# Loads of q and k head by head, one token per partition, ahead of the block transposes of an attention and MLP kernel

## The chip, the cores and the metric

The kernel runs on one core of a Trainium2 chip. The time is the device time of one execution in microseconds, the median of several runs: 353.92 us for the kernel before (3 runs, 352.54 to 354.34). TensorE (PE) multiplies matrices, VectorE (DVE) and ScalarE (ACT) work on elements, GpSimd (POOL) here mostly issues the loads that also cast fp32 to bf16, and SyncE (SP) issues the stores.

## The reference

Causal attention with a sliding window of 64 tokens, for 8 batches, 8 heads, 576 tokens and a head size of 64; its result, 4608 tokens of 512, goes through two dense layers with a SiLU between them.

```python
scores = (q @ k.transpose(0, 1, 3, 2)) / sqrt(64)
scores = where(0 <= i - j < 64, scores, -1e9)
attn = softmax(scores)
x = (attn @ v).transpose(0, 2, 1, 3).reshape(4608, 512)
h = x @ w_in                       # 512 -> 2048
out = (h * sigmoid(h)) @ w_out     # 2048 -> 512
```

All inputs and the output are fp32; the kernel computes in bf16 with fp32 accumulation.

## The kernel before

**Attention by batch.** A score matmul needs q and k with the head dimension on partitions. For batch 0 the transposes are done by TensorE (`turn_first`). For batches 1 to 7 they are done by VectorE in blocks of 32 by 32 (`turn_blocks`, L247): the head dimension is cut into two halves of 32, so that the four heads of a group fill 128 partitions, and the scores of one head are the sum of two matmuls over 32 rows (`scores`, L333). A batch has two groups of four heads (a = 0, 1), each with q and k, and each of these four tensors of [4 heads, 576 tokens, 64] takes one load (`load_four`, L240) into a buffer `nat` and two transposes, one per half of the columns.

The load of before gives partition p the p-th of 128 equal pieces of the flat tensor. 32 partitions hold one head, and a partition holds 18 consecutive tokens (NR = 18), 1152 elements in a row. Token number 18 t + r of a head lies in partition t of its 32, at row r. A block transpose takes one r, and its 32 output columns t belong to tokens 18 t + r, so they are written into `qt` or `kt` with a step of 18 elements.

After the scores of three blocks of 64 tokens for all 8 heads (a unit; three units a batch, g = 0 to 2) come the exponential on ScalarE (L339), a multiplication with the window's mask on VectorE (L342), the matmul with v (`values`, L351), the division by the row sums (`inverse` L358, `normal` L361), and a block transpose that puts the result into `bridge` with the model dimension on partitions (L365). v is loaded by GpSimd in four parts per batch (L254), and VectorE copies half of it by 64 partitions (`shift_v`, L299 and L301).

**The two dense layers by tile.** A tile is 512 tokens; there are nine. The first layer (L371) has 16 groups of four matmuls over 512 columns, each followed by a SiLU on ScalarE (L377); the second layer (L380) has four outputs of 16 matmuls each, each copied out (L386) and stored. Tile 0 splits its first FIRST = 8 groups into token ranges 0 to 192 and 192 to 512, so that work can begin when the first unit of batch 0 is done. A batch has 576 tokens, so tile j needs batches 0 to j, and of batch j only its first 512 - 64 j tokens.

**What sets the order.** The class `Plan` is a list scheduler that runs when the kernel is built. Each piece of work is added with a class, an assumed cost in microseconds on each engine that may do it, its dependences and, for PSUM users, a pool of banks. `Plan.run` simulates the engines with those costs and always takes the ready head of the class with the best rank. The result is a fixed order of instructions per engine; on the chip an engine waits at its next instruction, whatever stands behind it. The cost assumed for one block transpose is 0.7 us. Scores are held back by `scores_may_run` so that they stand between the second-layer matmuls of the tile before: during the second layer of tile j TensorE also does the scores and values of batch j + 1.

**Queues.** All loads except two go through GpSimd's one DMA queue in the order in which GpSimd issues them; there are eight semaphores for them, so an issue waits until the DMA eight places ahead has landed. At the start these are: q and k and v of batch 0, w_in in ten loads, then q and k of batch 1 (four loads), then w_out and v of batch 1 in the order of SECOND_LOADS = "wvvwvv" (w is one part of w_out, v one part of v) with the remaining parts of w_out, then q, k and v of batch 2 and so on. There are eight `nat` buffers, so the loads of batch b wait until the transposes of batch b - 2 have read theirs; there are two `qt` and two `kt`, so the transposes of batch b wait for the scores of batch b - 2; there are three buffers for v.

Of the kernel before, what the change touches and what calls it, by code (L numbers as in the profile page):

```python
# [122 lines left out]
def kernel(ctx, tc, q, k, v, w_in, w_out, out):  # L123
    nc = tc.nc
    B, H, S, D = q.shape
# [1 line left out]
    assert (B, H, S, D) == (8, 8, 576, 64) and (d_model, d_ff) == (512, 2048)  # L127
    NP = H // 2
    NB = S // 64
    NR = H * S * D // 2 // 128 // D  # L130
    NG = 3
    NDC = d_model // 128
    NFT = d_ff // 128
    TT = 512
# [1 line left out]
    TB = TT // 64  # L136
    NK = 2
    NN, NNB, NE, NOT, NGT = 8, 8, 12, 4, NFT + 3
    FIRST, SECOND_LOADS = 8, "wvvwvv"
    FIRST_LOADS = [(x[0], int(x[1])) for x in "q0 k0 q1 k1 q2 q3 k2 k3 v0 v1 v2 v3".split()]  # L140
    NOX, NRC, NV = 6, 6, 3
    NIV = 2
    NM0, MARGIN = 9, 1.3
# [16 lines left out]
    nats = [keep.tile([128, 2 * S], BF16, name=f"nat{i}") for i in range(NN)]  # L160
# [15 lines left out]
    p = Plan(  # L176
        {"at": range(4), "pv": range(4, 6), "mp": range(4, 8), "all": range(8)},
        rank=dict(prime=-8, early=-10, one=-9, first=-9, dma=-1, ld0=-1, st=-2, silu=-3, out=-2, pv=0, s=1, moe=99, warm=200, turn=2,
                  norm=0, inverse=0, bridge=0, exp=1, mask=1, lift=2, block=2, shift=2, cast=4, late=5, clear=9),
        rank0=dict(turn=-6, cast=-6, lift=-5, shift=-4.5, exp=-4, mask=-4, inverse=-3.5, norm=-3, bridge=-3.2),  # L180
        ahead=dict(s=-5.5, exp=-4.6, pv=-5.5, inverse=-4.3, norm=-4.2, bridge=-4.25),
    )
# [27 lines left out]
    def clear_vv(i):  # L210
        nc.vector.memset(vv[i][:, :, D:D + 1], 1.0)
        nc.vector.memset(vv[i][0:64, 0, 0:D], 0.0)
# [5 lines left out]
    c_vv = [p.add("one", {"DVE": 0.25}, lambda _, i=i: clear_vv(i)) for i in range(NV)]  # L218
# [17 lines left out]
        copies[e](out=natbs[w][:, 0:S], in_=nats[i][:, 0:2 * S].bitcast(FP32))  # L236


    def load_four(i, b, a, kk):
        nc.gpsimd.dma_start(  # L240
            out=nats[i], in_=(q, k)[kk][b, 4 * a:4 * a + 4].rearrange("h s d -> (h s d)").rearrange("(p x) -> p x", p=128))

    def turn_blocks(i, b, a, kk, part):

        n = NR // 2
        to = kt[b % NK][:, 64:] if kk else qt[b % NK]
        nc.vector.transpose(  # L247
            out=to[:, 2 * a * S:2 * a * S + 2 * S].rearrange("x (s t r) -> x r s t", s=2, r=NR)[:, n * part:n * part + n],
            in_=nats[i].rearrange("p (r s d) -> p r s d", r=NR, s=2)[:, n * part:n * part + n],
        )  # L250

    def load_v(e, b, part):
        g0, g1 = part * 9, part * 9 + 9
        queue[e].dma_start(  # L254
            out=vv[b % NV][:, 2 * g0 + 1:2 * g1 + 1:2, 0:D],
            in_=v[b].rearrange("h s d -> (h s) d").rearrange("(g p) d -> p g d", p=128)[:, g0:g1],
        )
# [7 lines left out]
    def load_w_out(f):  # L265
        nc.gpsimd.dma_start(
            out=w_out_sb[:, 2 * f:2 * f + 2, :],
            in_=w_out[f * 256:(f + 1) * 256, :].rearrange("(c p) m -> p c m", p=128),
        )
# [100 lines left out]
    def first_layer(bank, j, ft, c, lo, hi):  # L370
        nc.tensor.matmul(  # L371
            banks[bank["bank"][0]][:, lo:hi], lhsT=w_in_sb[:, c, ft * 128:(ft + 1) * 128],
            rhs=bridge[:, (j * TT + lo) // 64:(j * TT + hi) // 64, c], start=(c == 0), stop=(c == NDC - 1),
        )

    def silu(bank, gt, lo, hi):
        nc.scalar.activation(out=gts[gt][:, lo:hi], in_=banks[bank["bank"][0]][:, lo:hi], func=ACTF.Silu)  # L377

    def second_layer(bank, gt, m, f, lo, hi):
        nc.tensor.matmul(  # L380
            banks[bank["bank"][0]][:, 0:hi - lo], lhsT=gts[gt][:, m * 128:(m + 1) * 128], rhs=w_out_sb[:, f, lo:hi],
            start=(f == 0), stop=(f == NFT - 1),
        )
# [9 lines left out]
    win, wout = [], []  # L393
    v_landed = {}
    kq_done, v_done, s_last, pv_last = {}, {}, {}, {}
    nat_free = {}
    g_pv, g_norm, g_bridge, g_mask, o_done = [], [], [], [], {}
    moe = []
# [13 lines left out]
    n_nat = [0, 0]  # L412
# [30 lines left out]
    def add_w_out(which):  # L443
        wout.extend(p.add("dma", {"POOL": 0.75}, lambda _, f=f: load_w_out(f), dma=1.29, lat=MARGIN) for f in which)

    def add_batch_qk(b):
        busy = s_last.get(b - NK, []) + ([c_k[b % NK]] if b < NK else [])
        for a in range(2):
            kq_done[(b, a)] = []
            for kk in range(2):  # L450
                i = n_nat[0] % NN
                n_nat[0] += 1
                ld = p.add("dma", {"POOL": 0.66}, lambda _, i=i, a=a, kk=kk: load_four(i, b, a, kk), nat_free.get(i, []),
                           dma=1.7, lat=MARGIN)
                nat_free[i] = [p.add("block", {"DVE": 0.7}, lambda _, i=i, a=a, kk=kk, part=part: turn_blocks(i, b, a, kk, part),
                                     [ld] + busy, b=b) for part in range(2)]
                kq_done[(b, a)] += nat_free[i]
        if b < NIV:
            for n, what in enumerate(SECOND_LOADS):
                if what == "w":  # L460
                    add_w_out([len(wout)])
                else:
                    add_v_loads(b, [SECOND_LOADS[:n].count("v")], [c_vv[b]])

    def add_v_loads(b, parts, busy):
        v_landed.setdefault(b, []).extend(
            p.add("dma", {"POOL": 1.0}, lambda e, part=part: load_v(e, b, part), busy, dma=1.1, lat=MARGIN * (b > 0)) for part in parts)
# [61 lines left out]
    def add_tile(j):  # L529
        gt = {}  # L530
        for ft in range(NFT):
            gt[ft] = (n_gt[0] % NGT, [])
            n_gt[0] += 1
        work = [(ft, 0, TT) for ft in range(NFT)]
        if j == 0:
            work = [(ft, lo, hi) for lo, hi in ((0, 192), (192, TT)) for ft in range(FIRST)] + work[FIRST:]
        for i, (ft, lo, hi) in enumerate(work):
            have = [op for n in range((j * TT + hi + 191) // 192) for op in o_done[n]]
            g, si = gt[ft]
            bank = None  # L540
            for c in range(NDC):
                op = p.add("moe", {"PE": 0.0036 + (hi - lo) / 2400}, None,
                           have + win[ft] + (exps[0] if j == 0 else []), lat=0.1,
                           pool=None if c else "mp")
                bank = bank or op
                op["fn"] = lambda _, bank=bank, ft=ft, c=c, lo=lo, hi=hi: first_layer(bank, j, ft, c, lo, hi)
                moe.append((op, 1, 1 if c == 0 and (i == 0 or (lo, hi) != work[i - 1][1:]) else -1))
            si.append(p.add("silu", {"ACT": 0.18 + (hi - lo) * 0.00083}, lambda _, bank=bank, g=g, lo=lo, hi=hi:
                            silu(bank, g, lo, hi), [op] + free_gt.get(g, []), table="silu"))
            bank["untils"][0] = [si[-1]]  # L550
        order = [(m, f, 0, d_model) for m in range(4) for f in range(NFT)]
        if j == 0:
            order = [(m, f, 0, d_model) for f in range(NFT) for m in range(4)]
        if j == NTT - 1:
            order = order[:3 * NFT] + [(3, f, lo, hi) for lo, hi in ((0, 256), (256, 384), (384, 512)) for f in range(NFT)]
        bank, uses = {}, {}
        for i, (m, f, lo, hi) in enumerate(order):
            g = gt[f][0]
            op = p.add("moe", {"PE": 0.0036 + (hi - lo) / 2400}, None, gt[f][1] + [wout[f // 2]], lat=0.1,
                       pool=None if f else "mp")  # L560
            bank.setdefault((m, lo), op)
            op["fn"] = lambda _, bank=bank[(m, lo)], g=g, m=m, f=f, lo=lo, hi=hi: second_layer(bank, g, m, f, lo, hi)
            moe.append((op, 2, len(order) - i))
            uses.setdefault(g, []).append(op)
            if f == NFT - 1:
                ot = n_ot[0] % NOT
                n_ot[0] += 1
                cp = p.add("out", {"DVE": 0.18 + (hi - lo) / 1000, "ACT": 0.18 + (hi - lo) / 1160},
                           lambda e, bank=bank[(m, lo)], ot=ot, lo=lo, hi=hi: copy_out(e, bank, ot, lo, hi),
                           [op, free_ot.get(ot)])  # L570
                bank[(m, lo)]["untils"][0] = [cp]
                free_ot[ot] = p.add("st", {"SP": 0.45}, lambda _, ot=ot, m=m, lo=lo, hi=hi: store(ot, j, m, lo, hi), [cp],
                                    dma=0.75 * (hi - lo) / d_model)
        free_gt.update(uses)
# [63 lines left out]
```

The softmax here doesn't subtract the row's maximum and nothing guards it: scores larger than these inputs give would overflow.

## Time and profile before

| What | before |
|---|---|
| Time | 353.92 us |
| Span of the profiled execution | 352.9 us |
| TensorE busy | 305.3 us (87%) |
| VectorE busy | 233.8 us (66%) |
| ScalarE busy | 172.4 us (49%) |
| GpSimd busy | 65.1 us (18%) |
| Packets of the GpSimd queue | 47168, 18.06 MB written |
| Issues of q and k for batches 1 to 7 | 28 of 288 KB |
| Mean granted TensorE clock | 0.932 |

The profile's busy tenths cut the span into 40 slices of 8.8 us; a digit is the busy share in tenths. Lines of the groups name the source line, the engine, the operation, output and inputs, the shape and the count, then busy us and the mean ns of one, then the idle time of the engine just before and what ended it. Lines of the timeline begin with the start and the duration in us.

### The profile page before, as it was taken

To read this page: it belongs to the slowest core of one execution; us is meant where nothing else is said; L and a number is where in the kernel's file an instruction comes from. 1 tells how busy PE (TensorE), PEld (TensorE's weight loads), DVE (VectorE), ACT (ScalarE), POOL (GpSimd) and SP (SyncE) were. 2 spreads that over 40 slices of the span, in tenths; PEclk is the share of its full clock that TensorE was granted. 3 is DMA by queue.
4 is the path that set the end of the run, shared out by engine and by line. 5 is a ranking of instruction groups with operands and counts; after the bars stand their busy time and mean duration, and the time that the engine had idled before them with its cause. 6 is when DMAs were issued, how large, how long until landed. Compare 5 with 4: busy or idle time off the path is not lost.

```text
span 352.9 us, 8322 instructions
## 1 busy us (share of the span) xinstructions
PE 305.3 (87%) x3619; PEld 147.8 (42%) x3619; DVE 233.8 (66%) x328; ACT 172.4 (49%) x311; POOL 65.1 (18%) x93
## 2 busy tenths in 40 slices
PE   5959456989406999699989998999999999999996
PEld 2546123434103444344445443444444444444444
DVE  2648985999999699959998999699760262000000
ACT  5837333077301367335654675367547755614621
POOL 8946464001510051005000400000000000000000
PEclk9969969899855999789999998999999999999999
DMA  8999999363933192509451900100020011011002
GB/s 169 157 202 189 201 189 192 26 159 62 152 51 62 61 127 40 98 32 124 72 88 67 103 2 32 61 32 1 35 74 17 2 61 61 0 61 59 1 32 90
DMA packets 52965, 28.62 MB, mean 81 GB/s; under 512 B 38848, under 2 KB 44608, under 8 KB 52928
## 3 DMA queue, kind: packets, MB, share of 16 engines
q0 software_dynamic: 47168, 18.06, 44.5%
q1 hardware_dynamic: 5760, 10.03, 7.7%
q8 instruction: 28, 0.46, 0.5%
q14 instruction: 9, 0.07, 0.1%
HBM read 36.70 MB, written 9.44 MB: 131 GB/s over the span
## 4 chain that ended last, share of the span: by engine, by line
PE 46%; DVE 28%; issue 11%; DMA 7%; POOL 6%; ACT 1%; POOLq 0%; DVEq 0%; ACTq 0%
PE mp L380 26%; PE mp L371 15%; DVE qt L247 13%; DVE kt L247 11%; DMA vv<-in_v_dram 3%; DMA nat<-in_q_dram 3%; PE mp L351 3%; POOL vv L254 2%; PE at L333 2%; POOL w_in_sb L260 2%; DVE ox L361 1%; DVE bridge L365 1%; POOL natb L230 1%; DVE e L342 1%; POOL nat L240 1%
## 5 line engine op out<-in xcount | busy, mean ns | idle before, releaser
L380 PE MATMUL mp<-w_out_sb,g 128*128 128x512 bf16 (+2 forms) x608 | 138.6, 385 | 0.0
L371 PE MATMUL mp<-bridge,w_in_sb 128*128 128x512 bf16 (+2 forms) x608 | 130.5, 372 | 2.4 <-DVE ot L386 1.2
L377 ACT ACTIVATE g<-mp 128x512 bf16<-128x512 f32 (+2 forms) x152 | 86.0, 575 | 40.9 <-PE mp L371 39.8
L371 PEld LDWEIGHTS <-w_in_sb 128*128 128x128 bf16 x608 | 60.2, 99 | 71.2 <-issue 9.9
L380 PEld LDWEIGHTS <-g 128*128 128x128 bf16 x608 | 57.9, 101 | 67.2 <-issue 11.2
L247 DVE STREAM_TRANSPOSE qt<-nat 128x576 bf16<-128x576 bf16 x28 | 72.9, 2780 | 2.1 <-DMA nat<-in_q_dram 2.1
L247 DVE STREAM_TRANSPOSE kt<-nat 128x576 bf16<-128x576 bf16 x28 | 73.2, 2777 | 0.0
L386 ACT COPY ot<-mp 128x512 f32<-128x512 f32 (+2 forms) x37 | 20.6, 563 | 78.3 <-PE mp L380 57.8
L339 ACT ACTIVATE e<-at 128x384 bf16<-128x384 f32 x88 | 36.4, 496 | 43.9 <-PE at L333 43.8
L254 POOL DMA_DIRECT2D vv<-in_v_dram x32 | 32.4, 1021 | 46.1 <-PE mp L351 42.2
L342 DVE TENSOR_TENSOR e<-e,mask 128x384 bf16<-128x384 bf16 x84 | 25.1, 351 | 18.9 <-ACT e L339 18.6
L351 PE MATMUL mp<-vv,e 128*32 128x65 bf16 x888 | 13.8, 200 | 22.4 <-DVE e L342 21.8
L351 PEld LDWEIGHTS <-e 128*32 128x32 bf16 x1152 | 12.8, 98 | 40.8 <-DVE e L342 26.7
L365 DVE STREAM_TRANSPOSE bridge<-ox 128x384 bf16<-128x384 bf16 x48 | 24.8, 553 | 0.1
L358 DVE RECIPROCAL rc<-mp 128x6 f32<-128x6 f32 x37 | 7.1, 225 | 22.4 <-PE mp L351 21.7
L333 PE MATMUL at<-qt,kt 32*128 32x64 bf16 x1008 | 13.0, 196 | 9.0 <-DVE kt L247 8.6
L361 DVE TENSOR_TENSOR ox<-mp,rc 128x384 bf16<-128x384 f32 x37 | 18.4, 537 | 0.2
L240 POOL DMA_DIRECT2D nat<-in_k_dram x14 | 7.8, 554 | 46.5 <-DVE kt L247 37.5
L333 PEld LDWEIGHTS <-kt 32*128 32x128 bf16 x1008 | 10.2, 96 | 13.8 <-DVE kt L247 8.7
L240 POOL DMA_DIRECT2D nat<-in_q_dram x14 | 7.8, 554 | 35.9 <-DVE qt L247 19.4
L339 ACT ACT_TABLE_LOAD x7 | 9.0, 1283 | 9.2 <-PE at L333 9.1
L351 PE MATMUL at<-vv,e 128*32 128x65 bf16 x264 | 4.1, 201 | 6.8 <-issue 6.8
(50 smaller groups left out, 89.3 us busy)
## 6 DMA issues: line engine op xcount, KB each, us to landing
out_dram<-ot SPq DMA_DIRECT2D x35, 256.0 KB, 2.1
vv<-in_v_dram POOLq DMA_DIRECT2D x32, 144.0 KB, 5.7
nat<-in_q_dram POOLq DMA_DIRECT2D x14, 288.0 KB, 6.4
nat<-in_k_dram POOLq DMA_DIRECT2D x14, 288.0 KB, 4.5
w_out_sb<-in_moe_w_out_dram POOLq DMA_DIRECT2D x8, 256.0 KB, 9.1
w_in_sb<-in_moe_w_in_dram POOLq DMA_DIRECT2D x6, 256.0 KB, 8.9
w_in_sb<-in_moe_w_in_dram POOLq DMA_DIRECT2D x4, 128.0 KB, 5.3
natb<-in_q_dram POOLq DMA_DIRECT2D x3, 144.0 KB, 4.7
```

Of the source, the lines that this page charges most:

```text
L247: nc.vector.transpose(out=to[:, 2 * a * S:2 * a * S + 2 * S].rearrange("x (s t r) -> x r s t", s=2, r=NR)[:, n * part:n * part + n], in_=n ...
L254: queue[e].dma_start(out=vv[b % NV][:, 2 * g0 + 1:2 * g1 + 1:2, 0:D], in_=v[b].rearrange("h s d -> (h s) d").rearrange("(g p) d -> p g d", ...
L333: nc.tensor.matmul(at_six(op["bank"][h])[:, a, x], lhsT=kt[b % NK][r, at:at + 128], rhs=qt[b % NK][r, at:at + 64], start=(s == a == x == 0 ...
L339: nc.scalar.activation(out=es[n % NE], in_=at_six(bank), func=ACTF.Exp, scale=scale)
L342: nc.vector.tensor_mul(es[n % NE], es[n % NE], mask0 if g == 0 else mask)
L351: nc.tensor.matmul(at_pv(bank)[32 * h:32 * h + 32, x, t], lhsT=e_of(b, a, n, h)[:, x, 32 * t:32 * t + 32], rhs=vv[b % NV][:, (4 * a + h) * ...
L361: nc.vector.tensor_mul(oxs[n % NOX], at_pv(bank)[:, :, :, 0:D], rcs[n % NRC].unsqueeze(3).to_broadcast([128, 3, 2, D]))
L365: nc.vector.transpose(out=bridge[:, n0:n0 + 3, 2 * a:2 * a + 2].rearrange("x t s (u i) -> x t s u i", u=2), in_=oxs[n % NOX].rearrange("p ...
L371: nc.tensor.matmul(banks[bank["bank"][0]][:, lo:hi], lhsT=w_in_sb[:, c, ft * 128:(ft + 1) * 128], rhs=bridge[:, (j * TT + lo) // 64:(j * T ...
L377: nc.scalar.activation(out=gts[gt][:, lo:hi], in_=banks[bank["bank"][0]][:, lo:hi], func=ACTF.Silu)
L380: nc.tensor.matmul(banks[bank["bank"][0]][:, 0:hi - lo], lhsT=gts[gt][:, m * 128:(m + 1) * 128], rhs=w_out_sb[:, f, lo:hi], start=(f == 0) ...
L386: copies[e](out=ots[ot][:, lo:hi], in_=banks[bank["bank"][0]][:, 0:hi - lo])
```

## The change

`load_rows` replaces `load_four`. Each head is loaded by itself into its 32 partitions: partition p gets tokens p, 32 + p, 64 + p and so on, 18 rows of 64 elements. A block transpose of row r then gives the 32 consecutive tokens 32 r to 32 r + 31, and `turn_blocks` writes them as one run. The purpose is that the transposes write contiguous rows. The two transposes of a tensor still cover one half of the rows each. Where there was one DMA of 128 long rows there are now four of 32 x 18 rows of 64 elements.

The second part is the order of the loads of batch 1 and w_out: SECOND_LOADS is now "awbwvwvvwv", where a and b are q and k of the first and second four heads. The purpose is that w_out and v come as they are needed. The third part is the first layer: FIRST goes from 8 to 6, and tile 1 too splits its first six groups, into tokens 0 to 256 and 256 to 512. The planner's costs go to 0.75 us for a transpose and 0.72 us and 0.52 us for the issue and the data of a head.

```diff
-    NR = H * S * D // 2 // 128 // D
+    NR = S // 32
...
-    FIRST, SECOND_LOADS = 8, "wvvwvv"
+    FIRST, SECOND_LOADS = 6, "awbwvwvvwv"
...
-    def load_four(i, b, a, kk):
+    def load_rows(i, b, a, kk, h):
         nc.gpsimd.dma_start(
-            out=nats[i], in_=(q, k)[kk][b, 4 * a:4 * a + 4].rearrange("h s d -> (h s d)").rearrange("(p x) -> p x", p=128))
+            out=nats[i][32 * h:32 * h + 32].rearrange("p (r d) -> p r d", r=NR),
+            in_=(q, k)[kk][b, 4 * a + h].rearrange("(r p) d -> p r d", p=32))
...
         nc.vector.transpose(
-            out=to[:, 2 * a * S:2 * a * S + 2 * S].rearrange("x (s t r) -> x r s t", s=2, r=NR)[:, n * part:n * part + n],
-            in_=nats[i].rearrange("p (r s d) -> p r s d", r=NR, s=2)[:, n * part:n * part + n],
+            out=to[:, 2 * a * S:2 * a * S + 2 * S].rearrange("x (s r t) -> x s r t", s=2, r=NR)[:, :, n * part:n * part + n],
+            in_=nats[i].rearrange("p (r s d) -> p s r d", r=NR, s=2)[:, :, n * part:n * part + n],
         )
...
+        for what in SECOND_LOADS if b < NIV else "ab":
+            if what == "w":
+                add_w_out([len(wout)])
+            elif what == "v":
+                add_v_loads(b, [len(v_landed.get(b, []))], [c_vv[b]])
+            else:
+                add_four(b, "ab".index(what), busy)
+
+    def add_four(b, a, busy):
+        kq_done[(b, a)] = []
+        for kk in range(2):
+            i = n_nat[0] % NN
+            n_nat[0] += 1
+            ld = [p.add("dma", {"POOL": 0.72}, lambda _, i=i, kk=kk, h=h: load_rows(i, b, a, kk, h), nat_free.get(i, []),
+                        dma=0.52, lat=MARGIN) for h in range(4)]
+            nat_free[i] = [p.add("block", {"DVE": 0.75}, lambda _, i=i, kk=kk, part=part: turn_blocks(i, b, a, kk, part),
+                                 ld + busy, b=b) for part in range(2)]
+            kq_done[(b, a)] += nat_free[i]
...
         if j == 0:
             work = [(ft, lo, hi) for lo, hi in ((0, 192), (192, TT)) for ft in range(FIRST)] + work[FIRST:]
+        elif j == 1:
+            work = [(ft, lo, hi) for lo, hi in ((0, 256), (256, TT)) for ft in range(FIRST)] + work[FIRST:]
...
-                moe.append((op, 1, 1 if c == 0 and (i == 0 or (lo, hi) != work[i - 1][1:]) else -1))
+                moe.append((op, 1, 1 if c == 0 and (i == 0 or hi > work[i - 1][2]) else -1))
```

More of the change, by code (lines that the diff above doesn't have):

```diff
@@ L447, in add_batch_qk @@
         busy = s_last.get(b - NK, []) + ([c_k[b % NK]] if b < NK else [])
[L448 to L463, printed above, removed]
+        for what in SECOND_LOADS if b < NIV else "ab":
[15 more added lines that the diff above has]
+            kq_done[(b, a)] += nat_free[i]
     def add_v_loads(b, parts, busy):
```

## The prediction

> **What bounds the kernel now.** I read the busy tenths first, then the list of waits, the costliest groups, and the timeline of TensorE through each wait.
>
> ```profile
> PE   5959456989406999699989998999999999999996
> DVE  2648985999999699959998999699760262000000
> PEclk9969969899855999789999998999999999999999
> ```
>
> One digit is 8.8 us. From the sixth slice to the 27th VectorE is full, and where TensorE drops to 4, 5, 4 and 0 VectorE stands at 9. After slice 27 VectorE has free time and TensorE is full at full clock. So the first 230 us belong to VectorE and the rest to TensorE. What VectorE does there:
>
> ```profile
> L247 DVE STREAM_TRANSPOSE qt<-nat 128x576 bf16<-128x576 bf16 x28 | 72.9, 2780 | 2.1 <-DMA nat<-in_q_dram 2.1
> L247 DVE STREAM_TRANSPOSE kt<-nat 128x576 bf16<-128x576 bf16 x28 | 73.2, 2777 | 0.0
> L365 DVE STREAM_TRANSPOSE bridge<-ox 128x384 bf16<-128x384 bf16 x48 | 24.8, 553 | 0.1
> ```
>
> The 56 transposes of L247 are 146 of its 234 busy us. One takes 2.78 us for 576 columns, 4.8 ns a column; the same instruction at L365 needs 1.44 ns. L247 writes each element 18 elements from the last (`(s t r)` with r = 18 innermost in memory), L365 writes runs of 32 and reads with a step of 2. Two waits on TensorE's timeline show what that costs:
>
> ```profile
> 47.91 0.67 PE L333 MATMUL at<-qt,kt 32*128 32x64 bf16 x36 [8.57 <-DVE kt L247]
> ...
> 108.83 1.63 PE L351 MATMUL mp<-vv,e 128*32 128x65 bf16 x48 [16.73 <-DVE e L342]
> ...
> 111.15 6.22 PE L380 MATMUL mp<-w_out_sb,g 128*128 128x512 bf16 x18
> ...
> 156.04 4.06 PE L380 MATMUL mp<-w_out_sb,g 128*128 128x512 bf16 x18
> ```
>
> The first wait is for the transposes themselves. In the second the masks of batch 2 stand in VectorE's fixed order behind the eight transposes of batch 3. Eighteen matmuls after the wait take 6.22 us instead of 4.06: the granted clock was 0.64 in 111.0 to 117.3 us.
>
> I take a stage to be the time from one tile's first layer to the next. On the timeline L371 starts at 22.6, 71.7, 124.5, 162.5, 195.9, 231.0, 262.8 and 293.8 us. So the stages of tiles 0 to 6 last 49.1, 52.8, 38.0, 33.5, 35.1, 31.8 and 31.0 us, and tiles 7 and 8 with the end 59.1. A clean stage is 31.1: two layers of 64 matmuls at 14.0, and 2.9 of attention. The excess over clean ones is 18 + 21.7 + 6.9 + 2.4 + 4 + 0.7 = 54 us; that is the most there is to win.
>
> **What the Trainium skill says.** Vector Engine (DVE) Microarchitecture Reference, section "Measured stream behaviour on trn2": a port keeps its full rate only while elements come in runs of at least two adjacent 4-byte words, and a destination that steps 24 words costs 2.5 ns a column. The trace agrees in direction, with 4.8 ns for two-byte elements against 1.44. DMA: Bandwidth & Descriptors, section "Specifications": transfers under 512 B don't reach line rate. The trace agrees: loads of v write 128-byte packets at about 140 GB/s, loads of nat write 2304-byte packets at 207. SBUF — State Buffer, section "SBUF: two separate sides": GpSimd can't write descriptors while VectorE runs in a two-port mode. No run here shows that for transposes: issues of nat beside them took 528 to 616 ns. TensorE: Matmul & The Clock Gate, section "What's actually happening": idle TensorE falls to half clock and regains it when busy; the 6.22 us above agree.
>
> **Part 1: contiguous rows.** The new output pattern `(s r t)` has t = 32 innermost, the input runs 32 elements, and the size stays 128x576. The nearest row is L365. If everything scales, 553 x 576/384 = 0.83 us; if only the 192 added columns count at the 0.96 GHz of VectorE: DVE Perf Modes, section "Specifications", 0.553 + 0.20 = 0.75. I take 0.75 because some of the 553 ns is fixed. VectorE loses 56 x (2.78 - 0.75) = 114 us and has about 120 of work left; per batch 8 x 0.75 = 6 us instead of 22. With masks 4.2, reciprocals 1.3, norms 3.2, bridge 3.3 and shifts 1.5 that is 19.5 us in a 31 us stage. VectorE ceases to be a bound.
>
> **Part 2: four loads in place of one.** 28 loads of 128 packets become 112 loads of 32 x 18 = 576 packets of 128 bytes. Data: these lines are of the stretch 120 to 135 us, where four loads of v run with almost nothing beside them in the right half (0.375 us a slice):
>
> ```profile
> DMA  0000039400200089999999999999999962000000
> GB/s 0 0 0 0 0 147 399 153 0 0 44 0 0 0 55 114 145 96 171 274 257 172 157 135 144 135 134 149 172 183 198 188 96 35 14 12 12 12 0 0
> ```
>
> At 135 to 149 GB/s, about 1,100 packets a us, a head takes 0.53 us and four heads 2.1, against 294,912 B at 207 GB/s = 1.42 for the one load. A batch needs 16 x 0.53 = 8.5 us for q and k instead of 5.7, and 4 x 1.02 for v. Issue: 0.55 us is the row with 128 packets (L240), 1.02 that with 1152 (L254); between them I take 0.75. GpSimd then works 16 x 0.75 + 4.1 = 16 us per batch. Both lie beside TensorE's 31 us stage from batch 2 on and cost nothing there. GpSimd waits before an issue until the DMA eight places ahead has landed (its timeline: q and k of batch 1 go out at 16.9, 17.5, 19.4 and 21.7, then w_out and v wait one by one for the loads of w_in and nat). Queued behind those waits are w_out and v, for which tile 0's second layer and batch 1 wait. That is where Part 2 can show.
>
> **Part 3: the start, stage of tile 0.** w_in has landed by 26.8 (the issue at 26.79 waits for it). Eight heads follow at 0.53 (31.0), one w_out at 1.3, eight more heads at the issue pace of 0.75: all q and k of batch 1 by about 38, transposed by 39.5. Before, they landed by 32.4 and were transposed by 47.9. TensorE ends tile 0's first layer at 38.8 as before (it starts at 22.6 and runs 16.2 us), does nine second-layer matmuls, which the built order of the changed kernel puts ahead of the scores (2.0 us; before it was one) and wants the scores at 40.8. No wait, by 1.3 us. The mixed order lands v of batch 1 near 45 and the last w_out near 50; the values stand at 48 and the matmuls that need the last w_out after 53. End of the stage: 38.8 + 64 x 0.22 + 2.9 = 55.8, plus the 2.5 us stall at 58.0 of before, which no engine's result ends and which I leave in: 58.3, a stage of 35.7, 13.4 less.
>
> **Part 4: FIRST = 6 and tile 1 in two halves.** 16 more matmuls and four more activations, a few tenths of a us on TensorE and hidden on ScalarE (49% busy). In tile 1 the first 24 matmuls (0 to 256) can start before the last group's bridge, which hides most of the wait at 74.8 (1.23 us, for the copy of ot).
>
> **The sum.** Tile 0: 13.4. Tile 1: 52.8 to 32.3, 20.5: the 16.7 us wait, its slow clock and the 1.2 mostly go; batch 2 is loaded by about 60 and wanted at about 72. Tiles 2 to 6: 169.4 to 5 x 31.3 = 156.5, 12.9. In all 46.8; 353.9 - 46.8 = 307, and I say 308 for small new waits.
>
> **The rivals.**
> *GpSimd or the queue sets the start.* If a head costs as much as a whole v load (1.02 us), q and k of batch 1 land at 26.8 + 16.3 + 1.3 = 44.4, the scores wait 5 us and TensorE pays 2 to 3 for its clock; batch 2 is loaded 8 us later, by about 70, and may hold up tile 1's scores as well. 308 + 8 + 5 = 321. For it: the unseen 32-partition form and the wait on eight places. Against it: later stages have 15 us to spare.
> *The transposes gain only in part*, say 1.5 us: VectorE has 162 us, a stage needs 25.5, the start is 6 us later; 316.
> *Slower.* The step is not what makes L247 slow, or 32 partitions take a quarter of the engines. In the first case VectorE's chain stays as it is and begins up to 5 us later: 359. In the second a head takes 2.1 us, a batch 34 + 4 = 38, more than a stage: 26.8 + 7 x 38 + 62 for the last tiles and attention = 355 and more. Against it: L365 is the same instruction at 1.44 ns a column, and v has the same packets.
>
> **How the numbers follow.** Forecast 75%, GpSimd or queue 13%, transposes in part 6%, slower or equal 6%. Low end 301: the stall of 2.5, tile 0's slow first layer (16.2 against 14.0) and the small waits vanish as well. High end 323 takes in the first two rivals. Faster by over 0.5%: 94%; same 2%; slower 4%.
>
> **What would show it.** Right: rows of the transposes near 750 ns, VectorE near 120 us busy, no wait of TensorE over 3 us after 25 us, stages near 31 from tile 1 on, L371 of tile 1 starting near 58. Part 2 wrong: issues of nat near 1 us, or TensorE's scores at 41 waiting for a transpose that itself waits for a landing. Part 1 wrong: transposes above 1.2 us. The prediction also fails if a TensorE that is never idle is granted less clock than the 1.00 of 230 to 353 us.

## The result, and the profile after

The changed kernel takes 306.62 us (four runs, 305.89 to 307.19) against 354.03 us before (four runs, 352.54 to 354.34): a ratio of 0.867, with a 95% interval of 0.864 to 0.870. The forecast was 308 us in a range of 301 to 323.

These are the busy tenths of the changed kernel's page (40 slices, now of 7.6 us), and below them four of its costliest groups (busy us, mean ns of one, idle time before and what ended it):

```profile
PE   3959997999999999999999999999999999999996
DVE  2466457752999098806970786055204520000000
POOL 8967974969989997991230000000000000000000
PEclk9998999999999999999999999999999999999999
...
L240 POOL DMA_DIRECT2D nat<-in_k_dram x56 | 37.3, 679 | 11.6 <-DMA vv<-in_v_dram 4.6
L240 POOL DMA_DIRECT2D nat<-in_q_dram x56 | 37.9, 693 | 4.3 <-DMA vv<-in_v_dram 1.9
...
L248 DVE STREAM_TRANSPOSE qt<-nat 128x576 bf16<-128x576 bf16 x28 | 19.8, 746 | 4.1 <-DMA nat<-in_q_dram 4.1
L248 DVE STREAM_TRANSPOSE kt<-nat 128x576 bf16<-128x576 bf16 x28 | 19.7, 743 | 0.6 <-DMA nat<-in_k_dram 0.6
```

The holes in TensorE's row are gone after the seventh slice, and its granted clock is at nine tenths or more from the fifth on (mean of the span 0.994, before 0.932). VectorE's row is broken by zeros and fives: it has time to spare. GpSimd is now the one with a long row of nines: it loads ahead as far as the buffers let it and is done at 138 us. A transpose takes 0.745 us instead of 2.78.

TensorE's timeline at the two places where it waited before (first the scores of batch 1, then the values of batch 2 and the matmuls behind them; a wait would stand in brackets):

```profile
39.95 0.55 PE L334 MATMUL at<-qt,kt 32*128 32x64 bf16 x48
...
77.66 0.56 PE L352 MATMUL mp<-vv,e 128*32 128x65 bf16 x48
78.15 0.55 PE L334 MATMUL at<-qt,kt 32*128 32x64 bf16 x48
78.86 4.26 PE L381 MATMUL mp<-w_out_sb,g 128*128 128x512 bf16 x19 [0.16 <-issue]
```

No wait stands in front of either, and the 19 second-layer matmuls behind the second take 4.26 us; before, 18 took 6.22 at a granted clock of 0.64. The stages, from one tile's first layer to the next as the timelines start them:

| Stage of tile | before | forecast | after |
|---|---|---|---|
| start to the first | 22.6 | 22.6 | 22.8 |
| 0 | 49.1 | 35.7 | 35.0 |
| 1 | 52.8 | 32.3 | 31.6 |
| 2 to 6 together | 169.3 | 156.5 | 155.9 |
| 7, 8 and the end | 59.1 | 59.1 | 58.8 |

### The profile page after: what moved, and what is told of

Its sections match the earlier page's. It is cut to its first block, busy times and chain, and to the rows that moved or that the text cites. A ratio compares the mean times of both kernels' runs of the same rounds, so it can differ in the third digit from the quotient of the medians.

```text
span 304.1 us, 8450 instructions
## 1 busy us (share of the span) xinstructions
PE 286.7 (94%) x3601; PEld 144.1 (47%) x3635; DVE 136.9 (45%) x329; ACT 172.1 (57%) x314; POOL 125.4 (41%) x177
## 4 chain that ended last, share of the span: by engine, by line
PE 93%; issue 4%; DMA 2%; ACT 1%; ACTq 0%; POOLq 0%
PE mp L372 42%; PE mp L381 40%; PE at L334 3%; PE mp L352 3%; DMA natb<-in_q_dram 2%; PE at L352 1%; PE mp L586 1%; PE at L282 1%; PE mp L314 1%; PE at L586 0%; PE mp L322 0%; ACT e L340 0%; PE mp L282 0%; PE at L314 0%; ACT g L378 0%
## 5 line engine op out<-in xcount | busy, mean ns | idle before, releaser
L372 PE MATMUL mp<-bridge,w_in_sb 128*128 128x512 bf16 (+3 forms) x624 | 128.7, 364 | 0.5 <-ACT g L378 0.4
L381 PE MATMUL mp<-w_out_sb,g 128*128 128x512 bf16 (+2 forms) x574 | 124.5, 367 | 4.3 <-issue 3.7
L378 ACT ACTIVATE g<-mp 128x512 bf16<-128x512 f32 (+3 forms) x156 | 86.3, 564 | 36.6 <-PE mp L372 35.6
L381 PEld LDWEIGHTS <-g 128*128 128x128 bf16 x608 | 55.8, 98 | 60.9 <-issue 0.3
L340 ACT ACTIVATE e<-at 128x384 bf16<-128x384 f32 x88 | 36.5, 496 | 18.8 <-PE at L334 18.7
L240 POOL DMA_DIRECT2D nat<-in_k_dram x56 | 37.3, 679 | 11.6 <-DMA vv<-in_v_dram 4.6
L240 POOL DMA_DIRECT2D nat<-in_q_dram x56 | 37.9, 693 | 4.3 <-DMA vv<-in_v_dram 1.9
L248 DVE STREAM_TRANSPOSE qt<-nat 128x576 bf16<-128x576 bf16 x28 | 19.8, 746 | 4.1 <-DMA nat<-in_q_dram 4.1
L248 DVE STREAM_TRANSPOSE kt<-nat 128x576 bf16<-128x576 bf16 x28 | 19.7, 743 | 0.6 <-DMA nat<-in_k_dram 0.6
L359 DVE RECIPROCAL rc<-mp 128x6 f32<-128x6 f32 x37 | 6.9, 190 | 16.7 <-PE mp L352 16.0
L352 PE MATMUL mp<-vv,e 128*32 128x65 bf16 x888 | 10.4, 194 | 0.0
L302 DVE COPY vv<-vv 64x576 bf16<-64x576 bf16 (+1 forms) x13 | 7.2, 557 | 6.5 <-DMA vv<-in_v_dram 6.2
```

The source lines that it names most:

```text
L240: nc.gpsimd.dma_start(out=nats[i][32 * h:32 * h + 32].rearrange("p (r d) -> p r d", r=NR), in_=(q, k)[kk][b, 4 * a + h].rearrange("(r p) d ...
L248: nc.vector.transpose(out=to[:, 2 * a * S:2 * a * S + 2 * S].rearrange("x (s r t) -> x s r t", s=2, r=NR)[:, :, n * part:n * part + n], in ...
L340: nc.scalar.activation(out=es[n % NE], in_=at_six(bank), func=ACTF.Exp, scale=scale)
L352: nc.tensor.matmul(at_pv(bank)[32 * h:32 * h + 32, x, t], lhsT=e_of(b, a, n, h)[:, x, 32 * t:32 * t + 32], rhs=vv[b % NV][:, (4 * a + h) * ...
L372: nc.tensor.matmul(banks[bank["bank"][0]][:, lo:hi], lhsT=w_in_sb[:, c, ft * 128:(ft + 1) * 128], rhs=bridge[:, (j * TT + lo) // 64:(j * T ...
L381: nc.tensor.matmul(banks[bank["bank"][0]][:, 0:hi - lo], lhsT=gts[gt][:, m * 128:(m + 1) * 128], rhs=w_out_sb[:, f, lo:hi], start=(f == 0) ...
```

## The experiments

The parts of the change are tried apart: how the transposes write, how q and k are loaded, the order; then the planner's cost, and the margin of the new loads. My theory: VectorE's transposes were the bound, and everything else in the change is hidden or small. Its rivals: the order of loads or the smaller loads bring the gain; or the fault was an order planned with a cost of 0.7 us for work that takes 2.78.

**The write alone taken back** (`step_writes`), in the changed kernel:

```diff
-            out=to[:, ...].rearrange("x (s r t) -> x s r t", s=2, r=NR)[:, :, n * part:n * part + n],
+            out=to[:, ...].rearrange("x (s t r) -> x s r t", s=2, r=NR)[:, :, n * part:n * part + n],
```

> The changed kernel with its loads, order and planner's costs, but the transposes write with the step of 18 as before (so the columns of q and k in batches 1 to 7 stand in another order of tokens than the mask takes; the amount of work is the same). VectorE theory: a transpose takes 2.78 us again, VectorE is busy near 240 us, TensorE waits behind it, 350 to 362 us. Rival, the smaller loads or their order bring the gain: 305 to 320 us whatever the transposes take.

Measured: 344.4 us, a ratio to before of 0.976 (0.969 to 0.982). A group and a wait of it:

```profile
L248 DVE STREAM_TRANSPOSE qt<-nat 128x576 bf16<-128x576 bf16 x28 | 72.7, 2775 | 4.1 <-DMA nat<-in_q_dram 4.0
...
48.10 0.67 PE L334 MATMUL at<-qt,kt 32*128 32x64 bf16 x36 [8.76 <-DVE kt L248]
```

The 2775 ns are back with the output pattern alone, the input and the loads being the new ones, and with them 38 us and the 8.8 us wait. So the step of the write is the cause of the slow transposes, and these of the 38 us. The planner was told 0.75 us here too, so the 38 us hold both losses: the longer work, and an order planned for shorter work. The time is 6 us under my range, which took it for granted that VectorE's order doesn't matter. It does: here are masks of batch 2 with their neighbours in VectorE's order, first in the kernel before, then in this run.

```profile
103.32 5.27 DVE L247 STREAM_TRANSPOSE kt<-nat 128x576 bf16<-128x576 bf16 x2
108.24 1.33 DVE L342 TENSOR_TENSOR e<-e,mask 128x384 bf16<-128x384 bf16 x4
```

```profile
90.79 0.90 DVE L343 TENSOR_TENSOR e<-e,mask 128x384 bf16<-128x384 bf16 x3
91.61 5.11 DVE L248 STREAM_TRANSPOSE qt<-nat 128x576 bf16<-128x576 bf16 x2
```

Before, all eight transposes of batch 3 stand ahead of the masks; in this run the masks come first, and TensorE's longest wait for a mask is 4.4 us instead of 16.7. Which of the costs told to the planner brings this order was not tried alone.

**The loads alone taken back** (`one_load`): in the changed kernel, `load_four` of before and its one entry in the planner's list, with the contiguous write kept.

> The changed kernel with contiguous writes and its mixed order, but one load of 1152 elements per partition for four heads as before (so again the columns of q and k of batches 1 to 7 stand in another order of tokens than the mask takes; the amount of work is the same). VectorE theory, with loads hidden beside TensorE: 304 to 308 us, GpSimd near 65 us busy. Rival, the head loads cost time in the stage of tile 0: 300 us or less. Rival, head loads bring the gain: over 330 us.

Measured: 303.8 us, a ratio of 0.861 (0.856 to 0.866). GpSimd is busy for 65.4 us, the transposes take 0.74 us, and the stage of tile 0 lasts 33.6 us. Against the changed kernel's 0.867 (0.864 to 0.870) that is 2 to 3 us less, and the intervals overlap: four loads in place of one cost some 2 to 3 us, and they bring nothing. The profiled spans say where. Tile 1's first layer starts here, then in the changed kernel, at:

```profile
55.13 1.91 PE L371 MATMUL mp<-bridge,w_in_sb 128*128 128x256 bf16 x16
57.75 1.91 PE L372 MATMUL mp<-bridge,w_in_sb 128*128 128x256 bf16 x16
```

From there to the end both take 246.4 us. So the whole difference of 2.6 us lies ahead of tile 1. It is the price for tokens in the right columns.

**The order alone** (`order_only`): the kernel before with SECOND_LOADS = "awbwvwvvwv", FIRST = 6 and tile 1 in two halves.

> The kernel before with the mixed order of loads, FIRST = 6 and tile 1 in two halves alone; loads and transposes as before. VectorE theory: VectorE stays the bound, 348 to 360 us. Rival, the order of loads brings a good part of the gain: under 340 us.

Measured: 351.9 us, a ratio of 0.998 (0.996 to 1.001). The waits of 8.3 us for the transposes of batch 1 and of 14.1 us for the masks of batch 2 remain. The order brings nothing while VectorE is the bound.

**The layout alone** (`layout_only`): the changed kernel with the order, FIRST and the halves of tile 1 taken back.

```diff
-    FIRST, SECOND_LOADS = 6, "awbwvwvvwv"
+    FIRST, SECOND_LOADS = 8, "abwvvwvv"
...
-        elif j == 1:
-            work = [(ft, lo, hi) for lo, hi in ((0, 256), (256, TT)) for ft in range(FIRST)] + work[FIRST:]
```

> The changed kernel with loads by head and contiguous writes, but the order of before: q and k of batch 1 ahead of w_out and v, FIRST = 8, tile 1 in whole groups. VectorE theory: 306 to 311 us, the order being worth 0 to 4 us at the wait between tiles 0 and 1. Rival, the order is a large part: over 320 us.

Measured: 309.9 us, a ratio of 0.876 (0.871 to 0.882). Its timeline of TensorE shows what the order is for:

```profile
37.13 0.39 PE L381 MATMUL mp<-w_out_sb,g 128*128 128x512 bf16 x1 [0.60 <-DMA w_out_sb<-in_moe_w_out_dram]
40.92 1.02 PE L381 MATMUL mp<-w_out_sb,g 128*128 128x512 bf16 x4 [1.30 <-DMA w_out_sb<-in_moe_w_out_dram]
44.12 0.38 PE L381 MATMUL mp<-w_out_sb,g 128*128 128x512 bf16 x1 [0.73 <-DMA w_out_sb<-in_moe_w_out_dram]
```

With all sixteen heads ahead of w_out, tile 0's second layer waits for w_out in small pieces, 2.6 us in all, and its stage lasts 40.3 us instead of 35.0. Not all of that is w_out: the first layer of tile 0 has eight matmuls more here, and the stall among the values of batch 1, whose cause is open (see Part 3 below), is 2.56 us instead of 1.46, with 22 slow matmuls behind it in 6.59 us. The first layer starts 1.6 us earlier in this execution. With fast transposes the order, with FIRST and the halves, is worth 3 us of the whole; with slow ones it brought nothing, as `order_only` shows.

**The planner told the truth** (`true_cost`), in the kernel before:

```diff
-            return not whole and rest > 0 and not p.done(op["deps"])
+            return rest > 0 and not p.done(op["deps"])
...
-                nat_free[i] = [p.add("block", {"DVE": 0.7}, ...
+                nat_free[i] = [p.add("block", {"DVE": 2.78}, ...
```

> The kernel before with the planner told 2.78 us for a transpose in place of 0.7, so that masks stand ahead of most transposes in VectorE's order; scores may also run where the next tile's first layer has to wait, which the planner needs to end and which at 0.7 us leaves every engine's order as it was. VectorE theory: the work is too much wherever it stands, 28 us of start and some 225 us of VectorE ahead of the last scores, 335 to 352 us. Rival, the wrong order behind a wrong cost was the loss (the 16.7 us wait and its like): under 325 us.

Measured: 338.7 us, a ratio of 0.960 (0.953 to 0.967). Two starts of a first layer on TensorE's timeline:

```profile
103.72 1.91 PE L371 MATMUL mp<-bridge,w_in_sb 128*128 128x512 bf16 x8 [3.11 <-DVE bridge L365]
...
138.50 2.92 PE L371 MATMUL mp<-bridge,w_in_sb 128*128 128x512 bf16 x8 [3.12 <-DVE bridge L365]
```

The 16.7 us wait is gone, and in its place the first layers of tiles 1 to 4 wait 1.7 to 3.1 us for the bridge, which stands in the same VectorE queue; VectorE is busy 239.5 us. This order of the old work is worth 15 of the 47 us. The other 32 came with less work; that no order of the old work would save more is not shown, since only this one was tried.

**Twice as many issues** (`half_loads`), in the changed kernel:

```diff
-    def load_rows(i, b, a, kk, h):
-        nc.gpsimd.dma_start(
-            out=nats[i][32 * h:32 * h + 32].rearrange("p (r d) -> p r d", r=NR),
+    def load_rows(i, b, a, kk, h):
+        for x in range(2):
+            nc.gpsimd.dma_start(
+                out=nats[i][32 * h:32 * h + 32].rearrange("p (r d) -> p r d", r=NR)[:, 9 * x:9 * x + 9],
...
```

> The changed kernel with each head load cut into two of nine rows: 224 issues for q and k instead of 112, the same packets. Theory that issues are hidden beside TensorE with time to spare: a batch takes GpSimd 32 x 0.6 + 4 = 23 us of a 31 us stage, so only tile 0 pays, where the scores of batch 1 wait for the last head: 309 to 316 us. Rival, GpSimd's issues are near a bound already: over 325 us.

Measured: 334.4 us, a ratio of 0.948 (0.943 to 0.953): a clear miss. From its timelines, first TensorE's, then VectorE's ahead of the second wait:

```profile
46.78 0.58 PE L382 MATMUL mp<-w_out_sb,g 128*128 128x512 bf16 x1 [7.62 <-DMA w_out_sb<-in_moe_w_out_dram]
...
123.91 1.64 PE L353 MATMUL mp<-vv,e 128*32 128x65 bf16 x48 [5.12 <-DVE e L344]
```

```profile
117.62 1.44 DVE L249 STREAM_TRANSPOSE kt<-nat 128x576 bf16<-128x576 bf16 x2 [4.51 <-DMA nat<-in_q_dram]
122.18 1.44 DVE L249 STREAM_TRANSPOSE qt<-nat 128x576 bf16<-128x576 bf16 x2 [3.12 <-DMA nat<-in_q_dram]
123.54 1.12 DVE L344 TENSOR_TENSOR e<-e,mask 128x384 bf16<-128x384 bf16 x4
```

An issue takes 0.60 us (median), as assumed, and a batch 24 us of a 31 us stage. But the loads begin behind those of batch 1 and make up only 7 us a stage. The first wait is w_out behind 16 more issues (stage of tile 0: 45.5 us). The second is indirect: batch 4's transposes stand ahead of batch 3's masks in VectorE's fixed order, VectorE sits idle for loads that nobody needs yet, and TensorE waits for the masks. A third wait, 7.26 us for the masks of batch 5, is of the same kind. The stages of tiles 0, 2 and 4 are 10.6, 8.6 and 9.6 us longer than in the changed kernel, which is nearly all of the loss. What has to be spare is not GpSimd's time in a stage but the lead with which a load lands.

**The same, with the planner told of all issues** (`half_told`): 0.61 us of GpSimd and 0.26 us of data for each of the 224, and the planner's condition on scores as in `true_cost`.

> The kernel with head loads cut in two, with the planner told of all 224 issues (0.61 us each, 0.26 us of data), so that transposes of the next batch stand behind the masks where their loads come late; scores may also run where the next tile's first layer has to wait, which the planner needs to end and which leaves the changed kernel's order as it is. Theory that late landings cost only because VectorE's fixed order puts transposes ahead of masks: 312 to 322 us, no wait for masks over 3 us. Rival, GpSimd or the queue is simply full: 330 us or more.

Measured: 325.2 us, a ratio of 0.924 (0.919 to 0.928), 3 us over the range. No matmul waits more than 1.5 us for a mask any more. The 9 us won come with the order; of what remains, 10 us are in tile 0's stage (45.3 us) and 5 in tile 1's (36.4). There the scores of batch 1 wait 5.42 us for transposes whose loads land late, as the rival said of the queue.

**Two tokens per row** (`two_tokens`), to halve the number of packets without leaving the layout: `"(r p u) d -> p r (u d)"` with u = 2 in the load, and `"x (s r t u) -> x u s r t"` in the write. It was run beside the changed kernel (`after_again`) on one chip.

> The changed kernel with two consecutive tokens per row of a head load: 288 packets of 256 bytes a head instead of 576 of 128, and transposes that write with a step of 2, which the sweep of steps puts at 0.83 us against 0.76. Theory that the head loads cost a little, in tile 0's stage alone: issues near 0.6 us, 303 to 306 us, at or a little below the changed kernel. Rival, the step of 2 costs more beside the other work, or nothing hangs on the loads: 306 to 309 us.

> The changed kernel once more on this chip, for the comparison with two tokens per row: 305.5 to 307.5 us.

Measured: 306.1 us against 305.9. Issues fell from 0.69 to 0.64 us on average, transposes rose from 0.74 to 0.79, and nothing followed for the time. Half the packets are no gain, so the packets' number isn't what the 2 to 3 us ahead of tile 1 are paid for. `half_loads`, with the same packets in twice the issues, has 10.6 us more in tile 0's stage, so the issues are likelier; fewer issues with the same packets were not tried.

**A sweep of steps** (`step_sweep`): 14 transposes of 128x576 behind VectorE's last one. The output pattern is `"x (s t r) -> x s r t"` with r = 1, 2, 3, 6, 9 and 18, so that r is the step; L632 reads with a step of 18 and writes contiguously.

> The changed kernel with 14 more transposes of 128x576 on VectorE behind its last one, whose results nobody uses: output steps of 1, 2, 3, 6, 9 and 18 elements with contiguous input, and input step 18 with contiguous output, two of each. If the step of the write is what costs: 0.75 us at step 1, rising, 2.8 us at step 18; the strided read 0.75 to 1.6 us. If the order of a long run was the matter and not the step: steps 2 to 9 stay near 0.75 us. The time stays at about 306 us, since VectorE is idle there.

This is one execution, with two transposes of each kind. The span stays at 303.4 us, and the groups, by line (L620 is step 1, L622 step 2, L624 step 3, L626 step 6, L628 step 9, L630 step 18), give:

```profile
L628 DVE STREAM_TRANSPOSE nat<-nat 128x576 bf16<-128x576 bf16 x2 | 5.5, 2734 | 0.1
L630 DVE STREAM_TRANSPOSE nat<-nat 128x576 bf16<-128x576 bf16 x2 | 5.3, 2642 | 0.1
L626 DVE STREAM_TRANSPOSE nat<-nat 128x576 bf16<-128x576 bf16 x2 | 4.2, 2105 | 0.1
L632 DVE STREAM_TRANSPOSE nat<-nat 128x576 bf16<-128x576 bf16 x2 | 2.4, 1218 | 0.1
L624 DVE STREAM_TRANSPOSE nat<-nat 128x576 bf16<-128x576 bf16 x2 | 2.3, 1149 | 0.1
L622 DVE STREAM_TRANSPOSE nat<-nat 128x576 bf16<-128x576 bf16 x2 | 1.7, 830 | 0.1
L620 DVE STREAM_TRANSPOSE nat<-nat 128x576 bf16<-128x576 bf16 x2 | 1.5, 758 | 0.0
```

The write's step costs little at 2, half as much again at 3, and is at its worst at 9. The strided read costs 0.46 us where the same step on the write costs 1.88.

## Why the prediction was right, step by step

**What bounds the kernel.** Right, and shown by `step_writes` against the changed kernel: the output pattern alone moves 38 us. The limit of 54 us from clean stages held too; 48.8 us of the profiled span were won. They are not idle time alone: in `one_load`, whose trace has every matmul, TensorE is busy 290.2 us against 305.3 before, with 16 matmuls more, at a mean granted clock of 0.994 against 0.932. About 15 us of the gain are faster matmuls.

**Part 1.** A transpose was put at 0.75 us and took 0.745. The 0.75 was an estimate, and that it fits to 5 ns is partly luck: L365 also reads with a step of 2, where the new transposes read contiguous runs, so what is fixed in its 553 ns was not measured. VectorE's busy time was put near 120 us and is 136.9. The mis-sized term is 56 x 2.03 = 114 us: the means of neighbouring instructions overlap. Two slow transposes take 5.12 us on the timeline, not 5.56, and a full queue hides more of each record than one with gaps. By busy time of the groups the transposes lost 146.1 - 39.5 = 107 us, and the copies of v got about 2 us longer. Records of different groups overlap too: the groups of VectorE add up to 248.5 us before, of which the page counts 233.8, and to 144.3 and 136.9 after. That is another 7 us. Nothing hung on the difference.

**Part 2.** That the loads cost nothing from batch 2 on was right, as `one_load` shows: 246.4 us from tile 1 to the end with either load. The issue was put at 0.75 us and takes 0.69 on average. The data came slower than assumed: from 70.2 to 75.4 us, where eight heads are issued back to back, 4338 packets moved, 834 a us instead of 1,100, hence 0.69 us a head instead of 0.53. Whether the queue or the issues set that pace is open. The 207 GB/s read for nat were of a stretch (40 to 48 us) in which 917 of 1269 packets were under 2 KB, so not nat's alone; nothing hung on it. The reason given against the rival, that later stages have 15 us to spare, was not the right measure, as `half_loads` shows: with 7 us still to spare in a stage it lost 28 us. What saved the change is its lead. GpSimd ends the issue of the last head of batch 4 at 91.0 us, and the masks of batch 3, ahead of which batch 4's first transposes stand in VectorE's order, begin at 106.05:

```profile
89.07 1.96 POOL L240 DMA_DIRECT2D nat<-in_k_dram  x3 [0.27 <-issue]
...
106.05 1.50 DVE L343 TENSOR_TENSOR e<-e,mask 128x384 bf16<-128x384 bf16 x4 [7.24 <-ACT e L340]
```

**Part 3.** The scores of batch 1 were put at 40.8 us and stand at 39.95; the last transpose for them ends at 36.5, where 39.5 was forecast. Two terms were off, both to the safe side. The last head is issued by 32.7 and its transposes begin at 35.0, where all heads were to land by 38: the second eight go out from 27.05 on at 0.66 us each, not from 32.3 at 0.75. And tile 0's first layer does not end at 38.8 "as before" but at 37.7: FIRST = 6 takes eight of its 96 matmuls away, which Part 4 counted only in the net of 16 more. The stall, near 58 us before and left in at 2.5, came as 1.46:

```profile
50.89 0.31 PE L352 MATMUL at<-vv,e 128*32 128x65 bf16 x17 [1.46 <-issue]
```

Why it comes stays open; no engine's result ends it in either kernel. The traces give one hint: a packet of the profile's queue "instruction" moves about when it begins (from 58.2 to 59.2 us before, where the stall begins at 58.0; from 48.2 to 49.3 after, where it begins at 49.4), while the DMA engines are full of loads. That TensorE waits there for its instructions is a guess that no run isolates. Stage 0 as a whole came at 35.0 us where 35.7 was forecast; in another execution of the same kernel (`after_again`) it lasted 36.8, and a fit this close is partly luck.

**Part 4.** The 1.23 us wait within tile 1's first layer became 0.28.

**The rivals.** Partly faster transposes and a step that isn't the cause fell with the first row of the profile. That 32 partitions take a quarter of the engines fell with the eight heads issued in 5.2 us, 0.65 us each, where 2.1 would have been needed. GpSimd's queue as the bound of the start fell at this size, but for the 2 to 3 us of `one_load`, and came true at twice the issues, with 10 us in tile 0's stage. What I had not listed is that a part of the old loss was an order planned with a wrong cost: `true_cost` recovers 15 us of it. The forecast did not need it, because the changed kernel's planner is told 0.75 us and the transposes take 0.745.

## What to carry to other kernels

When one instruction takes several times what another form of it takes in the same trace, compare their access patterns before their sizes, and price the better form from the row that is there. Where a fixed order is planned from assumed costs, a wrong cost loses twice, once in time and once in the order; compare the planner's costs with the profile's means. Ask of a load that is moved or split not whether its engine has time in the stage, but which instruction in which queue waits for its landing, and how long before that it lands.

## What the runs showed of the hardware

A block transpose of 576 two-byte columns costs 0.76, 0.83, 1.15, 2.11, 2.73 and 2.64 us with output steps of 1, 2, 3, 6, 9 and 18 elements (`step_sweep`): it does not rise further from 9 to 18. With the step of 18 on the input instead, 1.22 us.

An issue of a casting load by GpSimd took 0.54 us with 128 packets, 0.60 with 288 (`half_loads`), 0.66 to 0.67 with 576 (medians of the changed kernel) and 1.02 with 1152. Up to 576 packets most of it does not depend on their number. Doubling the loads at equal packets therefore nearly doubled GpSimd's time for q and k, from 75.2 to 136.2 us. The number of packets is not all that counts: a load of w_out, with 256 rows of 1024 bytes, took 0.71 us (median of the kernel before).
